# Attention and two MoE layers on one core: the first two batches' attention as single-engine parts in a planned order

## Chip, core and metric

One Trainium2 chip, one core. The time is the device time of one execution in microseconds; the metric is the median of the runs. The engines are PE (TensorE matmuls), ACT (ScalarE), DVE (VectorE), POOL (GpSimd) and SP (SyncE, which here issues the DMAs).

## What is computed

```python
def _attn_ref(q, k, v, M_prev, z_prev, beta):        # B, H, S, D = 4, 8, 576, 64
    scores = scale * np.matmul(q, k.transpose(0, 1, 3, 2))
    scores = np.where(causal, -1000000000.0, scores)
    scores = scores - scores.max(-1, keepdims=True)
    a = np.exp(scores)
    a /= a.sum(-1, keepdims=True) + 1e-09
    local = np.matmul(a, v)
    def phi(x):
        return np.where(x > 0, x, np.exp(x) - 1.0) + 1.0
    q_p = phi(q)
    mem_ret = np.einsum('bhsd,bhde->bhse', q_p, M_prev)
    mem_norm = np.einsum('bhsd,bhd->bhs', q_p, z_prev)[..., None] + 1e-06
    mem_out = mem_ret / mem_norm
    g = 1.0 / (1.0 + np.exp(-beta))[None, :, None, None]
    return (g * mem_out + (1 - g) * local).astype(np.float32)

def _moe_ref(x, w_gate, w_val, w_out):               # 2304 tokens, 512 -> 1536 -> 512
    g = x @ w_gate
    return (g * (1.0 / (1.0 + np.exp(-g))) * (x @ w_val) @ w_out).astype(np.float32)

def _moe2_ref(x, w_in, w_out):                       # 512 -> 2048 -> 512
    h = x @ w_in
    return (h * (1.0 / (1.0 + np.exp(-1.702 * h))) @ w_out).astype(np.float32)
```

The attention's output, with its heads side by side, is the first layer's x, and that layer's output the second's.

## The kernel before

A *pair* is two heads of one batch; there are 16, four to a batch. For a pair, the queries are cut into four tasks k: k 0 is the first two blocks of 128 queries, k 1 and 2 one block each, k 3 the last 64 queries of both heads. Each task passes all engines: PE multiplies scores into a PSUM tile `s`; DVE masks them and takes the maxima (`nm`); ACT takes the Exp with its sums (`sm`) into `p`; DVE inverts the sums; POOL scales `p` (the norm); PE transposes it into a PSUM tile `tp`; ACT copies that to `pt`. When all four are there, PE multiplies `pt` with v, and phi with the memory M, into `o` (`av`), ACT copies `o` to `xh`, DVE subtracts for `xl` (a value in two parts). Beside this runs phi of the pair's queries `nq`: Exp on ACT, a maximum with zero on POOL (L246), a sum on DVE (L247), the product with z on POOL (L249), a row sum and reciprocal on DVE, a division on POOL (L262), transposes on PE and a copy on ACT. `prep_q` scales qk on POOL (L234) and lays the last 64 queries into `qt`.

The program has three stages. First, the attention of batches 0 and 1 (`attn` with `alone`, 8 pairs) with PSUM tiles from both pools by turns. Second, `moe` over batches 0 and 1, both layers, with the attention of batches 2 and 3 (8 pairs) woven in at a rate worked out from costs; its result goes to DRAM. Third, `second`, both layers over batches 2 and 3.

A weight chunk of 128x512 goes through four steps, on ACT, DVE and POOL and back: load, `dec_one` (a 64-bit number's bits made into fp32), `split_one` (the same value in two parts, `wp`), and a copy to DRAM for the third stage, for most chunks with four sums of quarters. Chunk 0 is asked for by `ahead(0)` in the first stage, after its 60th step, which pulls six loads, four decodes and three splits; `moe` takes one chunk after the other with `next_w`.

The order of the program's text is not the order on the engines: the scheduler places each instruction on its engine by its own simulated timeline, and each engine then works in that order, waiting where an input is missing. `alone` steps are appended by the rule

```python
for x in "osten" if alone else "etnso":
    acts[x]()
```

where o is `av`, s scores, t the transposes, e the Exp and n the norm of neighbouring tasks.

## Time and profile before

| | us |
|---|---|
| median of 3 runs | 1113.54 |
| lowest and highest run | 1113.03, 1114.75 |
| profiled execution | 1110.42 |
| its span | 1108.6 |

The profiled execution is a single one; its span runs from the first to the last instruction. PE is busy 1053.2 us of it, POOL 637.8, DVE 694.0 and ACT 528.4. An engine's busy time leaves out its waits; a wait is shown with what ended it. A row of the timeline merges neighbouring instructions of one kind.

### The profile page before, as it was taken

How to read it: one execution, taken by the hardware profiler on the slowest of the kernel's cores; microseconds unless marked ns; L12 is line 12 of the kernel's file. 1: busy time of each engine (PE TensorE's matmuls, PEld its weight loads, DVE VectorE, ACT ScalarE, POOL GpSimd, SP SyncE). 2: the span in 40 equal slices, each digit the busy share in tenths (PEclk: the TensorE clock that was granted, in tenths of full speed). 3: DMA queues.
4: the chain of work that ended last, by engine and by line, in shares of the span. 5: the costliest groups of instructions: out<-in, count | busy, mean ns of one | idle time of the engine just before them, and what ended most of it. 6: DMA issues, size and time to landing. Idle time of an engine off the chain costs nothing.

```text
span 1108.6 us, 19842 instructions
## 1 busy us (share of the span) xinstructions
PE 1053.2 (95%) x7664; PEld 972.6 (88%) x7664; DVE 694.0 (63%) x1077; ACT 528.4 (48%) x1075; POOL 637.8 (58%) x650
## 2 busy tenths in 40 slices
PE   4768889999999999999999999999999999999998
PEld 3445459999989998899999999999999999999998
DVE  6777646844765857674846644880754869175563
ACT  4666645544544554666636444442432436343230
POOL 8899755666767657575654633481753818152421
PEclk8888989999999999999999999999999999999999
DMA  5355322454354353343453417422122222222102
GB/s 204 95 185 158 103 60 74 165 173 157 121 182 156 114 186 134 119 171 122 151 162 105 170 57 257 167 100 77 67 90 88 75 86 84 78 87 89 53 24 86
DMA packets 46719, 133.94 MB, mean 121 GB/s; under 512 B 7584, under 2 KB 10400, under 8 KB 46624
## 3 DMA queue, kind: packets, MB, share of 16 engines
q1 hardware_dynamic: 46480, 132.67, 35.7%
q8 instruction: 60, 0.98, 0.4%
q14 instruction: 35, 0.29, 0.1%
q10 hardware_dynamic: 144, 0.00, 0.0%
HBM read 92.54 MB, written 40.11 MB: 120 GB/s over the span
## 4 chain that ended last, share of the span: by engine, by line
PE 55%; DVE 2%; POOL 1%; issue 1%; DMA 0%; SPq 0%; ACT 0%; POOLq 0%; ACTq 0%
PE m L86 51%; PE o L86 2%; PE s L86 1%; POOL wb L598 1%; PE tp L350 1%; DMA out<-ot 0%; SPq L813 0%; POOL wp L153 0%; DVE hl L468 0%; DVE phi L247 0%; DVE wa L142 0%; PE tp L362 0%; DVE xl L621 0%; POOL nq L246 0%; PE tphi L269 0%
## 5 line engine op out<-in xcount | busy, mean ns | idle before, releaser
L86 PE MATMUL m<-hh,wp 128*128 128x288 f32 x1792 | 313.0, 297 | 2.8 <-DVE acc L520 2.4
L86 PEld LDWEIGHTS m<-hh,wp 128*128 128x128 f32 x1792 | 262.3, 189 | 12.9 <-issue 5.9
L86 PE MATMUL m<-xh,wp 128*128 128x288 f32 x1280 | 237.3, 300 | 2.1 <-DVE acc L520 1.3
L598 POOL TENSOR_TENSOR wb<-raw,wb 128x256 fp32r<-128x256 f32 x140 | 126.5, 920 | 191.0 <-ACT wb L597 185.9
L86 PEld LDWEIGHTS m<-xh,wp 128*128 128x128 f32 x1280 | 191.1, 189 | 12.7 <-issue 4.8
L86 PE MATMUL m<-hl,wp 128*128 128x288 f32 x896 | 191.1, 296 | 0.0
L145 POOL TENSOR_TENSOR wa<-wa,wr 128x512 uint32<-128x512 uint32 x68 | 90.0, 1324 | 117.1 <-issue 65.2
L86 PEld LDWEIGHTS m<-hl,wp 128*128 128x128 f32 x896 | 143.7, 188 | 1.3 <-issue 1.3
L86 PE MATMUL m<-xl,wp 128*128 128x288 f32 x640 | 137.0, 296 | 0.0
L153 POOL TENSOR_TENSOR wp<-wa,wp 128x512 fp32r<-128x512 f32 x68 | 93.0, 1368 | 55.6 <-ACT wp L152 54.9
L86 PE MATMUL m<-xh,wb 128*128 128x288 f32 x640 | 119.0, 296 | 0.0
L86 PEld LDWEIGHTS m<-xl,wp 128*128 128x128 f32 x640 | 103.1, 189 | 0.0
L86 PEld LDWEIGHTS m<-xh,wb 128*128 128x128 f32 x640 | 96.9, 189 | 0.0
L597 ACT CAST wb<-raw 128x256 fp32r<-128x256 f32 x140 | 55.6, 404 | 78.8 <-PE m L86 77.2
L306 ACT ACTIVATE p<-s,nm 128x128 f32<-128x128 f32 (+3 forms) x128 | 66.0, 525 | 52.0 <-DVE nm L289 40.5
L86 PE MATMUL m<-th,wb 128*128 128x288 f32 x480 | 90.3, 296 | 0.0
L326 POOL TENSOR_SCALAR p<-p,sm 128x128 f32<-128x128 f32 (+3 forms) x128 | 76.0, 610 | 20.1 <-DVE sm L322 6.9
L139 DVE TENSOR_SCALAR wa<-wa 128x512 f32<-128x512 f32 x68 | 36.9, 544 | 74.8 <-ACT wa L138 73.7
L144 ACT ACTIVATE wr<-w 128x512 uint32<-128x512 uint16 x68 | 45.9, 675 | 71.9 <-POOL wa L145 71.5
L468 DVE TENSOR_TENSOR hl<-u,hh 128x576 fp32r<-128x576 f32 x56 | 59.2, 1056 | 28.2 <-ACT hh L467 27.7
L86 PEld LDWEIGHTS m<-th,wb 128*128 128x128 f32 x480 | 73.1, 189 | 0.0
L86 PE MATMUL m<-xl,wb 128*128 128x288 f32 x320 | 68.6, 296 | 0.0
(143 smaller groups left out, 1833.9 us busy)
## 6 DMA issues: line engine op xcount, KB each, us to landing
w<-w SPq DMA_DIRECT2D x40, 512.0 KB, 3.6
raw<-w SPq DMA_DIRECT2D x20, 896.0 KB, 4.6
w<-wo SPq DMA_DIRECT2D x28, 512.0 KB, 3.6
w<-wp SPq DMA_DIRECT2D x28, 512.0 KB, 2.7
wp<-w SPq DMA_DIRECT2D x28, 512.0 KB, 3.5
w<-sums SPq DMA_DIRECT2D x20, 512.0 KB, 2.9
qk<-qk SPq DMA_DIRECT2D x32, 288.0 KB, 3.7
nq<-nat SPq DMA_DIRECT2D x16, 320.0 KB, 3.5
```

The source lines that it names most:

```text
L86: nc.tensor.matmul(o, w, x, start=start, stop=stop)
L139: nc.vector.tensor_scalar(a, a, HIGH, LOW, op0=ALU.min, op1=ALU.max)
L144: nc.scalar.activation(r, rest, AF.Copy, scale=2.0 ** -13)
L145: nc.gpsimd.tensor_tensor(au, au, r, op=ALU.add)
L153: nc.gpsimd.tensor_sub(wp[:, 1], t, f(wp[:, 0]))
L306: mark[0] = nc.scalar.activation(p[:, j, c:c + n], s[:, j, c:c + n], AF.Exp, bias=nm[:, x, j:j + 1], accum_out=sm[:, x, j:j + 1])
L326: nc.gpsimd.tensor_scalar(p[:, j, c:c + n], p[:, j, c:c + n], sm[:, x, j:j + 1], 1.0, op0=ALU.mult, op1=ALU.mult)
L350: nc.tensor.transpose(t[:, j, c:c + 128], p[:, j, c:c + 128], ident)
L468: nc.vector.tensor_sub(hl, t, f(hh))
L597: nc.scalar.copy(wb[:, 0], src)
L598: nc.gpsimd.tensor_sub(wb[:, 1], src, f(wb[:, 0]))
```

## The change

The attention's functions are cut into parts that each run on one engine (`scores`, `top`, `expo`, `recip`, `norm`, `turn`, `turned`, and so on). For batches 2 and 3 (`beside`) the parts are called in the old sequence. For batches 0 and 1 (`alone`) each part becomes an entry with an engine, a duration, a priority, the parts it follows and the buffers that it takes and gives; `ordered` makes one order of them, starting on each free engine the ready part of lowest priority number; `pinned` then ties each instruction to the one before it on its engine, so that the scheduler can't move it. The first five weight loads and decodes and three splits are entries too, of the last priorities, and the loads wait for pair 7's first scores.

Some work differs as well, in all 16 pairs. phi's negative part is made by two ACT passes, exp(-relu(-q)), and its sum with max(q, 0) by one DVE pass; POOL's pass over nq is gone. The copy of `pz` moves from DVE to ACT. The reciprocals use a table `il2` without a broadcast. In the first stage `s` tiles have one PSUM pool and all others the second; qk has three buffers instead of two, p six instead of three, pt two of its own. The memory is laid out in stages: the first stage's tiles are freed before `up`, `hpool` and the second stage's are laid in their place; the decoding's tiles lie at the other end.

```diff
-            nc.scalar.activation(e, q, AF.Exp)
-            nc.gpsimd.tensor_scalar(q, q, 0.0, None, op0=ALU.max)
-            nc.vector.scalar_tensor_tensor(e, e, 1.0, q, op0=ALU.min, op1=ALU.add)
+            nc.scalar.activation(e, q, AF.Relu, scale=-1.0)
+            nc.scalar.activation(e, e, AF.Exp, scale=-1.0)
...
+            nc.vector.scalar_tensor_tensor(e, q, 0.0, e, op0=ALU.max, op1=ALU.add)
...
-                nc.vector.tensor_copy(pzs[i % 2][64:128], t[64:128, 1, 0:128].rearrange("p (j q) -> p j q", j=2))
+                nc.scalar.copy(pzs[i % 2][64:128], t[64:128, 1, 0:128].rearrange("p (j q) -> p j q", j=2))
...
+        def psum(name, score=False):
+            if alone and not score:
+                return ps_m.tile([128, 2, 512], F32, tag="m", name=name)
+            return ps_s.tile([128, 2, 512], F32, tag="s", name=name)
...
+    def ordered(ops, stock):
...
+            ready = sorted(
+                (key, n) for n, (e, us, key, after, takes, gives, do) in left.items()
+                if all(x in end and end[x] + (LAG.get(ops[x][0], 0.2) if ops[x][0] != e else 0.0) <= now for x in after))
+            for key, n in ready:
+                e, us, _, _, takes, _, _ = ops[n]
+                if e in used or any(stock[x] < 1 for x in takes):
+                    continue
...
+    def pinned(ops, order):
+        last = {}
+        for n in order:
+            traced = nc.cur_bb.bb.instructions
+            n0 = len(traced)
+            ops[n][6]()
+            for ins in nc.cur_bb.bb.instructions[n0:]:
+                prev = last.get(ins.engine)
+                if prev is not None:
+                    tc.add_manual_dep(
+                        ins, prev, mybir.DependencyInfo(mybir.DependencyClass.NoSync, mybir.DependencyReason.DATA),
+                        reason="order")
+                last[ins.engine] = ins.name
...
+                op("scores", w, (i, k), "PE", (0.95, 0.9, 1.06, 1.1)[k], (("prep_q", i),), ("s",),
+                   ("qk", "qt") if k == 3 else ())
+                op("top", w, (i, k), "DVE", (1.8, 1.4, 1.65, 1.0)[k], (("scores", i, k),))
...
+        wait = ("scores", NP - 1, 0)
...
+        for i in range(5):
+            key = 4 * NP + i
+            op("w", key, (i,), "SP", 0.4, (wait,), ("big",), do=load)
...
-    for n, (_, fn, args) in enumerate(attn(pairs[:2 * HP], True, direct)):
-        fn(*args)
-        if n == 60:
-            with tc.issue_after(mark[0].ins):
-                ahead(0)
-    steps = attn(pairs[2 * HP:], False, stage)
+    with tc.tile_pool(name="atta", bufs=1) as atta:
+        alone(atta, pairs[:2 * HP], direct)
+    up = ctx.enter_context(tc.tile_pool(name="up", bufs=3))
+    hpool = ctx.enter_context(tc.tile_pool(name="hpool", bufs=8))
...
+    steps = beside(attb, pairs[2 * HP:], stage)
```

How the order moves, at three places. PE before, around the output of pair 5 in the first stage (`s` scores, `tp` transposes of `p`, `o` output; 64x288 and the like are the parts of `o` from `pt`):

```order
L350 MATMUL tp<-ident,p 128x128 x8
L86 MATMUL s<-qk 128x384 x2
L86 MATMUL o<-ph,mz_97 128x288 x2
L362 MATMUL tp<-ident,p 128x128 x4
L363 MATMUL tp<-ident,p 128x128
L86 MATMUL s<-qk 128x512 x2
L350 MATMUL tp<-ident,p 128x128 x6
L86 MATMUL o<-pz_99,v 64x64 x2
L86 MATMUL o<-ptx,v 64x192 x2
L86 MATMUL o<-ptx,v 64x288 x6
```

PE now, around the outputs of pairs 3 and 4:

```order
L84 MATMUL s<-qk 128x384 x2
L380 MATMUL tp<-ident,p 128x128 x6
L84 MATMUL s<-qk 128x512 x2
L380 MATMUL tp<-ident,p 128x128 x8
L384 MATMUL tp<-ident,p 128x128 x4
L385 MATMUL tp<-ident,p 128x128
L84 MATMUL s<-qk,qt_87 128x288 x2
L380 MATMUL tp<-ident,p 128x128 x6
L84 MATMUL o<-ph,mz_88 128x288 x2
L84 MATMUL o<-pz_90,v 64x64 x2
L84 MATMUL o<-pt,v 64x192 x2
```

Before, the first two matmuls of `o` (with `ph` and mz) came ahead of the last transposes and of scores, and the rest of `o` after them; now `o` comes in one piece, and scores of the next pair and transposes stand between one `o` and the next.

ACT before, in the first stage at the weights' first decoding (L138, L144 decode, L152 splits, L306 is the Exp):

```order
L306 ACTIVATE p,sm<-s,nm 128x128 x2
L306 ACTIVATE p,sm<-s,nm 128x256 x2
L306 ACTIVATE p,sm<-s,nm 128x384 x2
L138 ACTIVATE wa<-w_565 128x512
L144 ACTIVATE wr<-w_565 128x512
L138 ACTIVATE wa<-w_567 128x512
L144 ACTIVATE wr<-w_567 128x512
L138 ACTIVATE wa<-w_569 128x512
L364 COPY ptx<-tp 128x2x4x64
L144 ACTIVATE wr<-w_569 128x512
L152 CAST wp<-wa 128x512
```

ACT now, at the end of the first stage (L343 and L347 are the Exp of pair 7, L142 and L143 decode, L425 makes `xh`, the others copy `tp`):

```order
L343 ACTIVATE p,sm<-s,nm 128x512 x2
L347 ACTIVATE p,sm<-s,nm 128x576
L142 ACTIVATE wa<-w_1202 128x512
L143 ACTIVATE wr<-w_1202 128x512
L142 ACTIVATE wa<-w_1204 128x512
L143 ACTIVATE wr<-w_1204 128x512
L425 CAST xh<-o 128x576
L398 COPY pt<-tp 128x2x3x128
L142 ACTIVATE wa<-w_1212 128x512
L143 ACTIVATE wr<-w_1212 128x512
L400 COPY pt<-tp 128x2x4x128
L402 COPY pt<-tp 128x2x4x64
```

The first decoding moved from among the third pair's Exps to behind the last pair's.

SP before, early in the first stage (w loads a weight, mz loads M into a tile that the pair two before it reads):

```order
L218 DMA nq<-nat 128x640
L226 DMA v<-nat 128x640
L229 DMA mz_97<-mem 64x64 x2
L119 DMA w_565<-w 128x1024
L119 DMA w_567<-w 128x1024
L119 DMA w_569<-w 128x1024
L218 DMA nq<-nat 128x640
```

SP now, at the end of the first stage (`w_92` is a weight's copy to DRAM; the last mz, qk, zb and nq are pair 8's):

```order
L117 DMA w_1202<-w 128x1024
L117 DMA w_1204<-w 128x1024
L117 DMA w_1212<-w 128x1024
L251 DMA mz_88<-mem 64x64 x2
L117 DMA w_1363<-w 128x1024
L176 DMA w_92<-wa 128x512
L117 DMA w_1395<-w 128x1024
L117 DMA w_1441<-w 128x1024
L251 DMA mz_89<-mem 64x64 x2
L229 DMA qk<-qk 128x576 x2
L238 DMA zb<-z 128x512
L240 DMA nq<-nat 128x640
```

The first weights' loads moved behind all eight pairs' loads, and those of pair 8 behind them.

POOL before, where the first stage ends (L333 and L326 norms, L234 and L237 prepare a pair's qk, L249 multiplies phi by z, L145 decodes, L153 splits):

```order
L234 TENSOR_SCALAR qk<-qk 128x576
L249 TENSOR_TENSOR nq<-phi,zb 128x640
L333 TENSOR_SCALAR p<-p,sm 128x576
L237 COPY qt_95<-qk 64x64 x2
L262 TENSOR_TENSOR phi<-phi,nrm 128x640
L326 TENSOR_SCALAR p<-p,sm 128x128 x2
L326 TENSOR_SCALAR p<-p,sm 128x256 x2
L153 TENSOR_TENSOR wp<-wa,wp 128x512
L145 TENSOR_TENSOR wa<-wa,wr 128x512
L153 TENSOR_TENSOR wp<-wa,wp 128x512
```

POOL now, in the same place, after the last norms (L258 and L261 prepare a pair's qk, L279 multiplies phi by z, L152 decodes, L171 splits, L180 to L183 sums):

```order
L152 TENSOR_TENSOR wa<-wa,wr 128x512 x2
L171 TENSOR_TENSOR wp<-wa,wp 128x512 x2
L180 TENSOR_TENSOR sums<-wa 128x256
L181 TENSOR_TENSOR sums<-sums,wa 128x256
L182 TENSOR_TENSOR sums<-wa 128x256
L183 TENSOR_TENSOR sums<-wa,sums 128x256
L152 TENSOR_TENSOR wa<-wa,wr 128x512
L258 TENSOR_SCALAR qk<-qk 128x576 x2
L261 COPY qt_86<-qk 64x64 x2
L279 TENSOR_TENSOR nq<-phi,zb 128x640
L261 COPY qt_87<-qk 64x64 x2
L171 TENSOR_TENSOR wp<-wa,wp 128x512
```

Before, the preparation of pairs 8 and 9 stood among the last norms of the stage, and four weights had been split ahead of them; now two weights are split after all norms, and the third weight's split stands behind that preparation.

## Rows read from the trace of the kernel before

**Rows 1.** The page's first part (busy us, share of the span, instructions) for PE, and its chain that ended last, by engine.

```profile
PE 1053.2 (95%) x7664; PEld 972.6 (88%) x7664; DVE 694.0 (63%) x1077; ACT 528.4 (48%) x1075; POOL 637.8 (58%) x650
...
PE 55%; DVE 2%; POOL 1%; issue 1%; DMA 0%; SPq 0%; ACT 0%; POOLq 0%; ACTq 0%
```

**Rows 2.** The table by stretches. Columns: the stretch and its length in us; busy us and instruction count of PE, PEld, DVE, ACT and POOL; granted TensorE clock; DMA share; GB/s.

```profile
20.00:158.00 138.00, 103.74 (x639) 64.45 (x638) 99.55 (x197) 87.45 (x218) 118.50 (x140) 0.87 0.41 125
158.00:200.00 42.00, 42.00 (x310) 38.88 (x310) 24.55 (x38) 18.88 (x37) 23.45 (x22) 0.97 0.23 71
200.00:665.00 465.00, 460.50 (x3402) 425.67 (x3401) 293.96 (x482) 246.97 (x475) 286.69 (x278) 1.00 0.43 144
101.95:149.21 47.26, 38.48 (x259) 24.43 (x259) 31.27 (x69) 29.99 (x80) 34.94 (x47) 0.93 0.32 98
116.91:131.66 14.75, 11.95 (x89) 7.51 (x88) 9.83 (x23) 10.35 (x28) 11.15 (x15) 1.00 0.34 105
```

**Rows 3.** PE's waits from 20 to 158 us: who waited for whom, us in total, times, longest.

```profile
PE o L86 <- ACT p L306: 14.6, 6, 4.5
PE tp L362 <- POOL p L333: 8.8, 5, 3.8
```

**Rows 4.** PE's timeline: start us, us, instructions merged by kind and count, and in brackets the idle time before them and what ended it. An `x8` of 64-row tiles is four matmuls of the program.

```profile
116.91 0.82 PE L350 MATMUL tp<-ident,p 128*128 128x128 f32 x6
...
124.23 1.24 PE L86 MATMUL o<-ph,mz 128*128 128x288 f32 x4 [2.46 <-ACT p L306]
...
131.66 1.14 PE L86 MATMUL s<-qk,qt 128*128 128x288 f32 x4
...
153.59 0.93 PE L86 MATMUL s<-qk 64*128 64x128 f32 x8
...
158.49 0.83 PE L86 MATMUL m<-xh,wp 128*128 128x288 f32 x2
...
162.85 2.83 PE L86 MATMUL o<-ptx,v 128*64 128x192 f32 x28
```

**Rows 5.** Groups of instructions from 101.95 to 149.21 us (three pairs), shapes kept apart: line, engine, operation, output<-inputs, shapes, count | busy us, mean ns of one | idle time before them and what ended it.

```profile
L246 POOL TENSOR_SCALAR nq<-nq 128x640 f32<-128x640 f32 x3 | 5.4, 1812 | 0.9 <-ACT phi L245 0.7
...
L295 DVE TENSOR_REDUCE nm<-s 128x1 f32<-128x576 f32 x3 | 2.3, 757 | 0.1
...
L245 ACT ACTIVATE phi<-nq 128x640 f32<-128x640 f32 x3 | 2.3, 756 | 0.0
...
L320 DVE SCALAR_TENSOR_TENSOR sm<-sm,il 128x4 f32<-128x4 f32 x3 | 2.1, 684 | 0.5 <-ACT p L306 0.5
...
L358 ACT COPY pt<-tp 128x1024 f32<-128x1024 f32 x2 | 2.0, 1012 | 0.0
...
L385 ACT CAST xh<-o 128x576 fp32r<-128x576 f32 x3 | 1.9, 641 | 0.4 <-PE o L86 0.3
...
L356 ACT COPY pt<-tp 128x768 f32<-128x768 f32 x2 | 1.6, 824 | 0.3 <-PE tp L350 0.3
...
L364 ACT COPY pt<-tp 128x512 f32<-128x512 f32 x2 | 1.2, 586 | 0.6 <-PE tp L363 0.5
...
L365 DVE COPY pz<-tp 64x128 f32<-64x128 f32 x3 | 0.9, 295 | 0.1
```

**Rows 6.** The first 20 us: the table by stretches for 14 to 20 (columns as above), then one row each of the timelines of SP's queue, ACT, POOL and PE.

```profile
14.00:20.00 6.00, 2.98 (x9) 2.30 (x10) 4.40 (x13) 3.23 (x12) 5.84 (x9) 0.50 0.42 144
6.14 0.58 SPq L218 DMA_DIRECT2D nq<-nat  x1
11.25 0.74 ACT L245 ACTIVATE phi<-nq 128x640 f32<-128x640 f32 x1 [2.61 <-DMA nq<-nat]
10.57 1.65 POOL L234 TENSOR_SCALAR qk<-qk 128x576 f32<-128x576 f32 x1
17.02 0.47 PE L350 MATMUL tp<-ident,p 128*128 128x128 f32 x1 [6.38 <-POOL p L326]
```

**Rows 7.** Groups of instructions from 160 to 665 us, the weights' decoding and splitting among them (columns as in rows 5).

```profile
L153 POOL TENSOR_TENSOR wp<-wa,wp 128x512 fp32r<-128x512 f32 x62 | 85.2, 1374 | 47.3 <-ACT wp L152 46.7
...
L145 POOL TENSOR_TENSOR wa<-wa,wr 128x512 uint32<-128x512 uint32 x61 | 80.7, 1323 | 115.2 <-issue 65.2 <-DVE sm L320 22.6 <-DVE wa L142 19.3
...
L142 DVE SCALAR_TENSOR_TENSOR wa<-w,wa 128x512 uint32<-128x512 uint32 x61 | 47.5, 779 | 1.1
...
L138 ACT ACTIVATE wa<-w 128x512 f32<-128x512 f32 x61 | 41.2, 675 | 45.0 <-POOL wp L153 44.8
...
L152 ACT CAST wp<-wa 128x512 fp32r<-128x512 f32 x62 | 38.2, 616 | 18.6 <-PE m L86 18.6
...
L139 DVE TENSOR_SCALAR wa<-wa 128x512 f32<-128x512 f32 x61 | 32.5, 533 | 73.7 <-ACT wa L138 72.6 <-DMA v<-nat 0.6
...
L164 POOL TENSOR_TENSOR sums<-wa 128x256 f32<-128x256 f32 x17 | 13.9, 821 | 0.0
```

**Rows 8.** From the page: the norm's passes on POOL in all 16 pairs (columns as in rows 5), and the loads of qk (line, engine, operation, count, KB each, median us from issue to landing); then POOL's timeline after the boundary.

```profile
L326 POOL TENSOR_SCALAR p<-p,sm 128x128 f32<-128x128 f32 (+3 forms) x128 | 76.0, 610 | 20.1 <-DVE sm L322 6.9
...
qk<-qk SPq DMA_DIRECT2D x32, 288.0 KB, 3.7
...
171.91 1.27 POOL L153 TENSOR_TENSOR wp<-wa,wp 128x512 fp32r<-128x512 f32 x1 [10.81 <-ACT wp L152]
```

**Rows 9.** DVE's timeline: a product on sm while the norms have not begun.

```profile
14.81 0.15 DVE L320 SCALAR_TENSOR_TENSOR sm<-sm,il 128x4 f32<-128x4 f32 x1
```

More of the change, by code (lines that the diff above doesn't have):

```diff
@@ L146, in dec_one, with two, three @@
+        def two():
+            nc.vector.tensor_scalar(a, a, HIGH, LOW, op0=ALU.min, op1=ALU.max)
+            nc.vector.tensor_scalar(au, au, 3, 0x3FFFFFFF, op0=ALU.logical_shift_left, op1=ALU.bitwise_and)
+            nc.vector.scalar_tensor_tensor(au, top, 0xC0000000, au, op0=ALU.bitwise_and, op1=ALU.bitwise_or)
+        def three():
+            nc.gpsimd.tensor_tensor(au, au, r, op=ALU.add)
         raws[i] = a
+        return one, two, three
     def split_one(i):
         upto("dec", i + 1, dec_one)
+        for stage in split_stages(i):
+            stage()
@@ L170, in ahead @@
+        return one, two
     def ahead(i):
@@ L388, in av, with beside @@
             done()
+        names = locals()
+        return {n: names[n] for n in (
+            "load_qk load_nq load_v prep_q phi_exp phi_sum phi_z phi_norm phi_div phi_turn phi_out scores top "
+            "expo recip norm turn turned av x_hi x_lo").split()}
+    def beside(pool, pairs, dest):
+        a = attention(pool, pairs, False, dest)
+        NP = len(pairs)
         tasks = [(i, k) for i in range(NP) for k in range(4)]
         NTK = len(tasks)
-        st, ptk = {}, {}
         steps = []
-        def add(cost, fn, *args):
-            steps.append((cost, fn, args))
@@ L398, in do_scores, with add @@
[L398 to L420 removed]
+        def add(cost, *what):
+            steps.append((cost, [(a[n], args) for n, *args in what]))
@@ L430, in attn @@
-            for x in "osten" if alone else "etnso":
-                acts[x]()
+            if 0 < t <= NTK:
+                add(0.0, ("expo", *tasks[t - 1]))
+            if 2 <= t < NTK + 2:
+                add(T_COST[tasks[t - 2][1]], ("turn", *tasks[t - 2]), ("turned", *tasks[t - 2]))
+            if 0 < t <= NTK:
+                add(0.0, ("recip", *tasks[t - 1]), ("norm", *tasks[t - 1]))
+            if t < NTK:
+                add(S_COST[k], ("scores", i, k), ("top", i, k))
+            if t >= 3 and tasks[t - 3][1] == 3:
+                x = tasks[t - 3][0]
+                add(3.9, ("av", x), ("x_hi", x), ("x_lo", x))
@@ L771, in tile_attention_moe_moe @@
     nc.vector.tensor_scalar(ig, ig, 1.0, None, op0=ALU.add)
+    for x in range(2):
+        nc.vector.tensor_copy(il2[:, :, x], il)
     for j in range(2):
```

355 lines of the change are left out of this document (211 added, 144 removed).

## The prediction

> **What bounds the kernel now.** I began with the page's busy shares and its chain of waits: PE is busy 95% of the span and carries 55% of the chain, nearly all of it the MoE matmuls [rows 1]. So work saved on another engine is worth something only where PE waits. The table by stretches says where that is [rows 2]. From 158 to 200 us PE is busy 42.00 of 42 us, from 200 to 665 us 460.50 of 465. From 20 to 158 us, in the first two batches' attention, it is busy 103.74 of 138 at a mean granted clock of 0.87: 34.3 us of idle PE, and PE work done in part at the lower of two clock levels. The change can win only there, and not more than some 45 us.
>
> Why PE waits there is in its waits [rows 3]: 14.6 us before the output matmul `o` on ACT, 8.8 us before the transposes of the last block on POOL. No engine is full: over three whole pairs without any weight decoding (101.95 to 149.21, 15.75 us each) PE is busy 38.48 of 47.26 us, POOL 34.94, DVE 31.27, ACT 29.99 [rows 2]. It is the order that makes 15.75 us of a pair. The row at 124.23 shows how: PE stands 2.46 us in front of `o` with transposes queued behind it [rows 4].
>
> **The floor after the change.** From 116.91 to 131.66 exactly one pair's PE instructions start, and PE is busy 11.95 us there at clock 1.00 [rows 2, 4]. POOL has 34.94 / 3 = 11.65 per pair and loses the pass over nq, 1.81 [rows 5]: 9.84. DVE has 10.42 and loses the copy of pz, 0.30: 10.1. ACT has 10.0 and gains the Relu pass and that copy. The trace has no Relu; bounds are 0.64 and 0.82, ACT passes over 576 and 768 elements, and I take the 0.76 of the Exp on the same tile. For the copy I take DVE's 0.30; ACT's 0.59 for 128x512 is the upper bound [rows 5]. ACT: 11.1. So PE leads with 11.95 and ACT follows at 93% of that. The other edits (il2 filled at the start by two tiny copies on an idle DVE; deeper rings for qk, p and pt) add nothing to a busy engine.
>
> **The ramp.** PE starts with the first pair's scores and then idles 6.38 us; from 14 to 20 us its clock is 0.50; the first transpose starts at 17.02 [rows 6]. The new order keeps that chain. The second nq load, issued at 6.14, is used at 11.25, and ACT needs it for two passes before the first Exp of scores; pair 1's qk is scaled from 10.57 [rows 6]; then POOL does the phi products, a division and the first norm in a row, with the nq passes gone. I take 17.5 us for the first transposes, 0.5 later than now for the second ACT pass.
>
> **The stretch.** 8 x 11.95 = 95.6, less 3.9 for the scores done in the ramp (a third of a pair), plus 2.0 for a restart at half clock (14 to 20 holds 2.98 us of PE [rows 6], the new order puts more there): 93.7 us of PE work. PE will not be full. The nearest rows are 81%, the three pairs in the old order, and 100%, 158 to 200 us, where all inputs lie ready [rows 2]. I choose 93%, nearer to the upper: the two waits that made most of the gaps are in-order waits, and PE's new order runs up to three score tiles ahead and no longer splits `o` around other work; but ACT at 93% of PE's load can't serve every slot. 93.7 / 0.93 = 100.8; the ends are 93.7 and 115.7.
>
> **The tail.** After the last scores of pair 7 PE still has one `o` (1.24 + 2.83 [rows 4]) and 19 transposes (0.82 for six): 6.7 us. Beside it go DVE's maximum, 0.76, an Exp like that of phi, 0.76, and then on ACT, by the new order, three weight decodes of two passes (6 x 0.675), x_hi (0.64) and four PSUM copies (0.82, 1.01, 0.59, 0.30) before the last `o` can start [rows 5, 7]: 8.9. So 2.2 us idle. The stage ends at 17.5 + 100.8 + 2.2 = 120.5 us (113.4 to 135.4).
>
> **What it is compared with.** Now the first MoE matmul starts at 158.49, with the last `o` (2.83 from 162.85) still to come and 0.9 us of pair 8's scores (153.59) already done [rows 4]. For the same PE work the old boundary is 158.49 + 2.83 - 0.93 = 160.4. Gain 39.9 us.
>
> **What comes back.** The five weight decodes that lay in the middle of this stage come at its end, and pair 8's loads queue among theirs on SP. Let E be the stage's end. Weights 0 and 1 are loaded well ahead; each then takes ACT 1.35, DVE about 1.8 (0.53, a like pass, 0.78), POOL 1.32, ACT 0.62, POOL 1.37 [rows 7], and they are ready about 1 us before and 1 us after E, where PE needs the second at E + 5.9. Weight 2's last pass stands on POOL behind four sums (0.82 each) and behind the scaling of pairs 8 and 9. Their loads follow on SP a mem load into a tile that pair 7's `o` still reads: they leave from E + 2 on and land, 3.7 us each [rows 8], near E + 6 and E + 8. Then come the second scaling, qt, a phi product, qt and the pass, some 5.6 us of POOL: weight 2 is whole near E + 14, and PE wants it after two weights and pair 8's first score tiles, also near E + 14. Weight 3 (E + 21) is level with its use as well. POOL has 10.81 us of idle there now [rows 8]; it will have none. I take 2 us of new stall, between 0 and 8 (two loads later by as much as one takes). After that PE is full as before [rows 2], and ACT's added 1.1 us per pair lie beside it, where ACT is busy 246.97 of 465 us; uncovered they would cost 9 us.
>
> Gain 39.9 - 2 = 37.9. The profiled execution took 1110.42 us, so 1072.5 after. The runs' median, 1113.54, lies 3.1 above it: I predict **1076 us**.
>
> **Where the Trainium skill speaks.** PE's pause before 17.02 is followed by 0.50 of clock from 14 to 20 us [rows 6]. The Trainium skill's page "TensorE: Matmul & The Clock Gate" (Part 1: The HAM clock gate) says that the array is throttled by default and that activity releases it. By that rule each gap left in the new order costs twice, which is the mechanism of the first rival.
> DVE's product on sm takes 0.15 us at 14.81 [rows 9] and 0.68 on average in the three pairs [rows 5]. The Trainium skill's page "GPSIMD Engine Reference" (1. Specifications) says that POOL shares its SBUF interface with VectorE and contends with instructions of two SBUF inputs. The slow rows agree; by that rule a denser order makes DVE's work longer, the second rival.
>
> **Rivals.**
> 1. *The gaps stay, and the low clock with them.* In-order waits on the two `m` buffers, with six users per pair, leave a pair at the 15.75 us of the three pairs, whose clock is 0.93 [rows 2]. 93.7 us are 7.84 pairs: 123.5, end 143.2, gain 160.4 - 143.2 - 2 = 15: 1098. For it: ACT is nearly as loaded as PE. Against: the old gaps stand before two named waits.
> 2. *DVE becomes the bound.* If each of the four sm products and their reciprocals takes 0.5 us more: 10.1 + 2 = 12.1 per pair, level with PE. Two full engines instead of one at a share of 88%: 106.5, 5.7 later than forecast: 1082.
> 3. *The weights come too late.* The whole 8 us of stall: 1082, and 1085 with a spell of half clock after it.
> 4. *Slower than now.* One pinned order makes one late load stop all that is behind it. On SP the z row of batch 1 is issued ahead of pair 4's qk and must wait until POOL has multiplied pair 3's phi by z; in POOL's order pair 4's scaling then follows after eight norm passes (8 x 0.61 = 4.9 us [rows 8]) and a division, while the load needs its issue and 3.7. If such a ring formed in every pair, the gain is nothing at (158.4 - 19.7) / 7.84 = 17.7 us a pair, and at 19 us the time is 1124. Against it: that wait is met once, and the work before the scaling about covers it.
>
> **How the numbers follow.** Forecast (PE bound, share 88 to 100%, stall 0 to 4): 0.70, with a range of its own from 1063 to 1083. Rival 1, and what lies between it and 1083: 0.15. Rivals 2 and 3: 0.07. Rival 4: 0.06, of which 0.05 is slower. Better than 1063: 0.02. The range 1063 to 1096 reaches to rival 1's near half and so holds some 0.84. A difference of 0.2% (2.2 us) is what a measurement can tell from none: faster 0.93, same 0.02, slower 0.05.
>
> **What would show it.** Right: the first MoE matmul near 121 us; PE's share from 20 to 115 us above 88% at a clock of 0.97 or more; `o` no longer waiting for an Exp; at most 2 us of idle PE in the 40 us after the boundary. Wrong: a clock under 0.95 in that stretch (rival 1), DVE busier than PE (rival 2), PE waiting before the first weights' matmuls on POOL's wp (rival 3), PE waiting on pair 4's scaling (rival 4), or a MoE part, from its first matmul to the end, that is not within 3 us of the 948 us that 1108.6 - 160.4 makes it now.

## The result and the profile after

| | before | after |
|---|---|---|
| median, us | 1113.28 (1112.48 to 1114.75) | 1087.49 (1085.24 to 1088.78) |
| profiled execution, its span | 1110.42, 1108.6 | 1085.24, 1083.4 |
| after / before | | 0.9765 (0.9743 to 0.9786) |

The change is faster by 2.35%, within the forecast range of 1063 to 1096 and 11.5 us above the point 1076. The page's first part and its chain, as in [rows 1] (busy us, share, instructions):

```profile
PE 1039.8 (96%) x7664; PEld 967.1 (89%) x7664; DVE 690.2 (64%) x1063; ACT 542.1 (50%) x1107; POOL 612.6 (57%) x634
...
PE 54%; DVE 3%; DMA 1%; ACT 1%; POOL 1%; issue 1%; SPq 0%; DVEq 0%; POOLq 0%
```

PE's busy time fell by 13.4 us (the same 7664 matmuls, at a mean granted clock of 0.998 instead of 0.980), the span by 25.2; the rest is idle time of PE. The table by stretches says where, with the columns of [rows 2]: the stage from its first transposes to the first MoE matmul, its middle, the 72.5 us behind it, and the long part:

```profile
22.52:127.48 104.96, 90.70 (x669) 59.22 (x668) 77.62 (x166) 84.59 (x215) 74.48 (x103) 1.00 0.31 96
34.60:113.40 78.80, 71.39 (x522) 46.48 (x522) 58.47 (x130) 62.16 (x165) 57.56 (x84) 1.00 0.31 97
127.48:200.00 72.52, 64.44 (x444) 58.99 (x442) 58.60 (x84) 40.43 (x83) 64.05 (x60) 0.98 0.59 195
200.00:640.00 440.00, 437.90 (x3236) 406.13 (x3237) 274.79 (x448) 241.45 (x465) 267.69 (x263) 1.00 0.43 145
```

Three readings. In the middle of the stage PE is busy 71.39 of 78.80 us (91%) at clock 1.00, against 81% at 0.93 in the old order's three pairs [rows 2]. From 200 us on it is full, as before. Between, 8.1 of 72.5 us are idle; in the 72.5 us behind the first MoE matmul of the kernel before it was 0.7.

PE's waits from 22 to 128 us, beside [rows 3] (who waited for whom, us in total, times, longest):

```profile
PE s L84 <- ACT p L343: 6.4, 9, 1.6
PE tp L380 <- issue: 1.9, 2, 1.6
PE tp L380 <- DVE xl L430: 1.7, 1, 1.7
PE tp L380 <- ACT ph L303: 1.1, 1, 1.1
PE tp L380 <- POOL qk L258: 1.0, 1, 1.0
PE o L84 <- ACT pt L400: 0.7, 1, 0.7
```

The 14.6 us of `o` behind an Exp and the 8.8 us of the last transposes behind POOL are gone. What is left is one small wait met often: scores for a free `s` tile, which an Exp still reads. PE's timeline at the ends of the stage, beside [rows 4, 6]:

```profile
18.43 2.08 PE L84 MATMUL s<-qk 64*128 64x512 f32 x4 [9.18 <-ACT p L343]
...
22.52 0.79 PE L299 MATMUL tphi<-ident,phi 128*128 128x128 f32 x5
...
121.10 1.07 PE L380 MATMUL tp<-ident,p 128*128 128x128 f32 x8 [1.73 <-DVE xl L430]
...
123.39 1.24 PE L84 MATMUL o<-ph,mz 128*128 128x288 f32 x4 [0.68 <-ACT pt L400]
...
127.48 0.53 PE L84 MATMUL m<-xh,wp 128*128 128x288 f32 x2
```

The first transposes start at 22.52, where I had said 17.5, and the first MoE matmul at 127.48, where I had said 120.5; no `o` is left behind it. From there to the end are 1083.4 - 127.48 = 955.9 us, which I call the MoE part below; before it was 948.2 by the count of the prediction. So the profiled execution is 12.7 us above the forecast 1072.5: 5.0 in the ramp, 2.0 in stretch and tail, 5.7 in the MoE part.

**The ramp.** DVE's timeline from 9 to 18 us:

```profile
9.70 0.83 DVE L273 SCALAR_TENSOR_TENSOR phi<-nq,phi 128x640 f32<-128x640 f32 x1 [3.40 <-ACT phi L268]
13.06 1.84 DVE L273 SCALAR_TENSOR_TENSOR phi<-nq,phi 128x640 f32<-128x640 f32 x1 [2.54 <-ACT phi L268]
14.82 0.69 DVE L327 TENSOR_TENSOR s<-s,bound 128x512 f32<-128x512 f32 x1
15.54 1.02 DVE L329 TENSOR_REDUCE nm<-s 128x2 f32<-128x256 f32 x2
```

PE's first scores ended at 9.25, but DVE masks them only at 14.82: in its order phi's sum of pair 1 stands in front, and that waits for ACT, which waits for pair 1's nq. SP issued nq at 5.56, ACT took it at 11.52: 6.0 us, for which the plan's table has 2.0 (`LAG`). The PE row at 18.43 is the end of that: 9.18 us idle before the third task's scores.

**Behind the boundary.** DVE's and ACT's timelines, and PE's waits from 127 to 200 us:

```profile
131.50 0.79 DVE L146 TENSOR_SCALAR wa<-wa 128x512 f32<-128x512 f32 x1 [2.48 <-ACT wa L142]
...
138.56 0.83 DVE L273 SCALAR_TENSOR_TENSOR phi<-nq,phi 128x640 f32<-128x640 f32 x1 [4.00 <-ACT phi L268]
139.31 0.75 DVE L645 SCALAR_TENSOR_TENSOR u<-u,m 128x576 f32<-128x576 f32 x1
140.14 1.77 DVE L146 TENSOR_SCALAR wa<-wa 128x512 f32<-128x512 f32 x1
```
```profile
137.02 0.74 ACT L267 ACTIVATE phi<-nq 128x640 f32<-128x640 f32 x1 [4.44 <-DMA nq<-nat]
```
```profile
PE m L84 <- DVE u L654: 3.5, 3, 1.8
PE m L84 <- DVE u L645: 3.2, 5, 1.5
PE s L84 <- ACT p L347: 1.4, 1, 1.4
```

PE doesn't wait for a weight (`wp`), as the prediction had it, but for DVE's `u`, which has to empty the PSUM tile of the product before. And DVE is not free for it: it stands 4.0 us before pair 8's phi, whose nq landed late, and then works without a pause, with decoding passes between the `u`.

### The profile page after: what moved, and what is told of

It reads as the page before. It is cut to its first block, busy times and chain, and to the rows that moved or that the text cites. A ratio compares the mean times of both kernels' runs of the same rounds, so it can differ in the third digit from the quotient of the medians.

```text
span 1083.4 us, 19848 instructions
## 1 busy us (share of the span) xinstructions
PE 1039.8 (96%) x7664; PEld 967.1 (89%) x7664; DVE 690.2 (64%) x1063; ACT 542.1 (50%) x1107; POOL 612.6 (57%) x634
## 4 chain that ended last, share of the span: by engine, by line
PE 54%; DVE 3%; DMA 1%; ACT 1%; POOL 1%; issue 1%; SPq 0%; DVEq 0%; POOLq 0%
PE m L84 50%; PE o L84 1%; PE s L84 1%; DVE hl L615 1%; DMA raw<-w 1%; PE tp L380 1%; DMA xr<-x 0%; DVE u L685 0%; ACT hh L614 0%; POOL wa L152 0%; DVE xl L768 0%; DMA x<-st 0%; DVE wa L149 0%; POOL p L368 0%; POOL wp L171 0%
## 5 line engine op out<-in xcount | busy, mean ns | idle before, releaser
L84 PE MATMUL m<-xh,wp 128*128 128x288 f32 x1280 | 239.9, 302 | 6.7 <-DVE u L645 3.2
L152 POOL TENSOR_TENSOR wa<-wa,wr 128x512 uint32<-128x512 uint32 x68 | 92.7, 1364 | 105.3 <-issue 48.5
L171 POOL TENSOR_TENSOR wp<-wa,wp 128x512 fp32r<-128x512 f32 x68 | 93.5, 1375 | 40.6 <-ACT wp L168 40.2
L146 DVE TENSOR_SCALAR wa<-wa 128x512 f32<-128x512 f32 x68 | 42.2, 620 | 77.3 <-ACT wa L142 76.8
L343 ACT ACTIVATE p<-s,nm 128x128 f32<-128x128 f32 (+3 forms) x128 | 66.1, 530 | 32.6 <-DVE nm L329 30.5
L84 PE MATMUL s<-qk 64*128 64x128 f32 (+3 forms) x256 | 54.2, 487 | 23.3 <-ACT p L343 15.0
L142 ACT ACTIVATE wa<-w 128x512 f32<-128x512 f32 x68 | 46.1, 677 | 58.2 <-POOL wp L171 52.9
L143 ACT ACTIVATE wr<-w 128x512 uint32<-128x512 uint16 x68 | 46.1, 677 | 53.6 <-POOL wa L152 53.2
```

The lines of the kernel that those rows point to most:

```text
L84: nc.tensor.matmul(o, w, x, start=start, stop=stop)
L142: nc.scalar.activation(a, top.bitcast(F32), AF.Abs)
L143: nc.scalar.activation(r, rest, AF.Copy, scale=2.0 ** -13)
L146: nc.vector.tensor_scalar(a, a, HIGH, LOW, op0=ALU.min, op1=ALU.max)
L152: nc.gpsimd.tensor_tensor(au, au, r, op=ALU.add)
L171: nc.gpsimd.tensor_sub(wp[:, 1], t, f(wp[:, 0]))
```

## The experiments

All times are medians in us, the ratio is to the kernel before, timed on the same chip beside it, with its 95% interval; the chips differ between rows, so the ratios compare better than the medians. "First" is the first MoE matmul of the profiled execution, "MoE part" its span less that, "u" PE's waits for DVE's `u` in the 72.5 us behind it, "decoded" the chunks whose decoding was complete before it (POOL's last pass, L152).

| kernel | median | ratio | first | MoE part | u | decoded |
|---|---|---|---|---|---|---|
| before | 1113.28 | | 158.49 | 950.1 | 0.7 | 7 |
| after | 1087.49 | 0.9765 (0.9743 to 0.9786) | 127.48 | 955.9 | 6.7 | 2 |
| phi alone | 1106.58 | 0.9946 (0.9926 to 0.9966) | 159.91 | | 0.5 | 7 |
| no ties | 1092.76 | 0.9826 (0.9788 to 0.9863) | 141.35 | 948.7 | 4.6 | 7 |
| weights early | 1092.19 | 0.9818 (0.9786 to 0.9851) | 141.82 | 950.0 | 3.2 | 7 |
| shallow buffers | 1101.25 | 0.9894 (0.9877 to 0.9912) | 151.16 | 946.8 | 1.5 | 5 |
| minimum on DVE | 1085.98 | 0.9756 (0.9738 to 0.9775) | 132.14 | 952.8 | 8.5 | 3 |
| DVE's order | 1082.47 | 0.9734 (0.9705 to 0.9763) | 131.90 | 948.6 | 3.1 | 4 |
| less DVE decoding | 1080.69 | 0.9708 (0.9694 to 0.9722) | 127.38 | 951.4 | 4.6 | 2 |
| less POOL | 1086.59 | 0.9759 (0.9742 to 0.9777) | 127.66 | 957.2 | 9.5 | 2 |
| nq first | 1084.96 | 0.9750 (0.9724 to 0.9776) | 126.56 | 956.4 | 8.5 | 2 |
| nq first, less DVE | 1083.94 | 0.9721 (0.9687 to 0.9755) | 127.52 | 954.7 | 6.4 | 2 |
| less DVE and POOL | 1082.87 | 0.9722 (0.9688 to 0.9756) | 127.59 | 953.3 | 6.6 | 2 |
| three edits | 1081.16 | 0.9720 (0.9697 to 0.9743) | 122.06 | 956.0 | 7.0 | 2 |

(Before, 1.9 us of attention matmuls stood behind the first MoE matmul, hence 950.1 here and 948.2 in the prediction; with phi alone `o` stands behind it too, and the MoE part can't be compared.)

**phi alone.** The kernel before, with the new phi in all 16 pairs and nothing else:

```diff
-            nc.scalar.activation(e, q, AF.Exp)
-            nc.gpsimd.tensor_scalar(q, q, 0.0, None, op0=ALU.max)
-            nc.vector.scalar_tensor_tensor(e, e, 1.0, q, op0=ALU.min, op1=ALU.add)
+            nc.scalar.activation(e, q, AF.Relu, scale=-1.0)
+            nc.scalar.activation(e, e, AF.Exp, scale=-1.0)
+            nc.vector.scalar_tensor_tensor(e, q, 0.0, e, op0=ALU.max, op1=ALU.add)
```

> The kernel before, with phi alone changed, in all 16 pairs: two ACT passes in place of one on ACT and one on POOL. Theory (order, not POOL's load, made a pair 15.75 us): gain of 0 to 6 us, 1107 to 1113. Rival (POOL's pass over nq held the first stage): gain of 12 us or more, 1101 or less.

0.54% (0.34 to 0.74), some 6 us of the change's 26, come from the cheaper phi, the upper end of the theory's 0 to 6. The rest lies in the other edits together: the order, the buffers, the two PSUM pools, the copy of pz and `il2`.

**No ties.** The plan and the buffers of the change, but the scheduler may move instructions:

```diff
-                if prev is not None:
+                if False:
```

> The changed kernel, with the parts written in the planned order but the instructions not tied to their predecessors, so that the scheduler places them. Theory (the order on the engines is what gained): much of it is lost, first MoE matmul at 140 to 155, time 1098 to 1112. Rival (the cut into parts, the buffers and the order of writing are enough): within 3 us of 1087.

Neither: 1092.8, some 5 us lost of 26. The first transposes come at 20.83, but the first MoE matmul 14 us later. From 34.60 to 113.40 us, against the row above:

```profile
34.60:113.40 78.80, 64.65 (x434) 41.32 (x434) 64.85 (x131) 60.86 (x156) 74.87 (x97) 0.96 0.41 131
```

POOL is busy 74.87 of 78.80 us instead of 57.56: without ties the scheduler put seven weights' decoding into the stage, four of them into this stretch. So what the ties keep seems to be mostly one thing: they hold the decoding at the stage's end. The next run, which keeps the ties and moves the decoding alone, ends in the same place.

**Weights early.** The same by the plan itself, with ties: the loads wait for pair 3's scores, with priorities among the pairs':

```diff
-        wait = ("scores", NP - 1, 0)
+        wait = ("scores", 3, 0)
...
-            key = 4 * NP + i
+            key = 16 + 3 * i
             op("w", key, (i,), "SP", 0.4, (wait,), ("big",), do=load)
```

> The changed kernel, with the five weights' loads waiting for pair 3's first scores instead of pair 7's, and their priorities spread over pairs 4 to 7. Theory (the 8.1 us that PE idles in the 72.5 us after the boundary come from decoding that is caught up there on a full POOL and DVE): that idle falls to 2 or less, the first MoE matmul comes 5 to 8 us later, time 1085 to 1090. Rival (the idle comes from pairs 8 and 9, whose preparation starts in the same place, or from the memory's reuse): idle stays at 6 or more and the time rises by the 5 to 8 us, to 1092 to 1096.

It ends as the run without ties did: stage 14.3 us longer, twice what I expected, MoE part 5.9 us shorter. The idle behind the boundary falls from 8.1 to 3.6 us, between the two expectations, and the time is the rival's. The two runs give the exchange rate: decoding inside the stage, where POOL then fills (71.29 of 78.80 us here), costs about twice what it saves behind it.

**Shallow buffers.**

```diff
-            t = new("qk", [128, 2, S], 3 if deep else 2)
+            t = new("qk", [128, 2, S], 2)
...
-            p = ps[i, k] = new("p", [128, 2, 512], 6 if deep else 3)
+            p = ps[i, k] = new("p", [128, 2, 512], 3)
...
-        order, us = ordered(ops, {"qk": 3, ..., "p": 6, ...
+        order, us = ordered(ops, {"qk": 2, ..., "p": 3, ...
```

> The change with the old depth of buffers in the first stage: qk two instead of three, p three instead of six (pt stays). Theory (PE's share of 91% in 34 to 113 us rests on scores and Exps running ahead of the transposes, for which p and qk have room): with three p each Exp waits for an older transpose, s tiles are freed later, PE's waits for s grow from 6.4 us; first MoE matmul 5 to 12 us later than 127.5, time 1091 to 1098. Rival (the order alone does it; the two s tiles bind and not p): first MoE matmul within 2 us of 127.5, time 1085 to 1090.

More than expected: 13.8 us, with the first MoE matmul 23.7 us later and the MoE part 9.1 us shorter. PE's waits for `s` grow from 6.9 to 12.8 us (the Exps of all tasks). In the middle of the stage PE's share falls from 91% to 83%, and the plan, with fewer free buffers, now sets two splits and four sums on POOL ahead of the last norms, before which PE stands 6.96 us:

```profile
34.60:113.40 78.80, 65.21 (x457) 42.55 (x459) 52.83 (x118) 55.58 (x145) 55.06 (x78) 0.96 0.27 81
```
```profile
139.69 1.97 PE L380 MATMUL tp<-ident,p 128*128 128x128 f32 x8 [6.96 <-POOL p L368]
```

So the gain of the order stands on room to run ahead. Without it an order from the same planner is worth half, though a part of what is lost is the decoding that it moved ahead of the norms. The old order with the new buffers and PSUM pools was not run: what the room alone is worth isn't shown.

**Minimum on DVE.** ACT relieved of one phi pass per pair (in the plan it is a part of its own, on DVE):

```diff
-            nc.scalar.activation(e, q, AF.Relu, scale=-1.0)
-            nc.scalar.activation(e, e, AF.Exp, scale=-1.0)
+            nc.vector.tensor_scalar(e, q, 0.0, None, op0=ALU.min)
+            nc.scalar.activation(e, e, AF.Exp)
```

> In all 16 pairs phi's first pass, the Relu on ACT, becomes a minimum with zero on DVE (0.7 us); the Exp and the sum stay as they are in the change. ACT's load in the stage goes from 84.6 to about 78, DVE's from 77.6 to about 83. Theory (PE's idle 14% of the stage is waiting for ACT's Exp, 'PE s from ACT p', because ACT is nearly as full as PE): those waits fall from 6.4 us to 3 or less, first MoE matmul 3 to 6 us earlier, and the first pair's phi ends 0.8 us sooner; time 1081 to 1085. Rival (the load of ACT does not matter, the waits are those of a round trip through DVE, ACT and two score tiles): nothing in the stage, and DVE's added 0.7 us per pair makes the first chunks after the boundary later; time 1087 to 1091.

The waits for `s` behind that Exp do fall, from 6.4 to 2.4 us. But the first MoE matmul comes 4.7 us later and the time is that of the change within its error: the plan came out with decoding ahead of pair 7's last norms, and PE stood 6.03 us before them. The middle of the stage:

```profile
34.60:113.40 78.80, 72.67 (x512) 46.84 (x512) 56.35 (x130) 58.40 (x157) 55.48 (x78) 0.96 0.32 99
```

Its 72.67 us are not more work than the 71.39 of the change: they hold 512 matmuls instead of 522, at a mean granted clock of 0.96 instead of 1.00. So what ACT's load costs in the stage isn't shown by this run. The next one speaks against a large part, for there the same waits fall to 3.3 us with ACT's work as it was.

**DVE's order.** One more dependency in the plan, pair 1's phi sum behind pair 0's second maximum:

```diff
-            op("phi_sum", t - 0.5, (i,), "DVE", 0.85, (("phi_exp", i),))
+            op("phi_sum", t - 0.5, (i,), "DVE", 0.85,
+               (("phi_exp", i),) + ((("top", 0, 1),) if i == 1 else ()))
```

> The changed kernel, with one dependency more in its plan: DVE's phi sum of pair 1 comes after the maxima of pair 0's first two tasks instead of ahead of them. Theory (the plan counts 2.0 us from a load's issue to its use, the trace shows 6.0 for pair 1's nq, so DVE stands 2.5 us before that sum with pair 0's scores ready): the first Exp of scores starts near 13.1 us instead of 16.66, PE's first transposes near 18.5 instead of 22.52, the first MoE matmul near 124 instead of 127.5, time 1083 to 1085. Rival (the loads and POOL's preparation bound the start whatever DVE does): first transposes stay within 1 us of 22.5, time 1086 to 1089.

The ramp is settled: transposes 4.1 us earlier, by one instruction's place.

```profile
18.40 0.71 PE L299 MATMUL tphi<-ident,phi 128*128 128x128 f32 x5
```

The time fell by 5.0 us, a little more than expected, but not by the way expected: the first MoE matmul came 4.4 us later and the MoE part was 7.3 us shorter, since the plan, with other times at its start, set two chunks ahead of the last norms. POOL and PE there:

```profile
115.60 2.69 POOL L171 TENSOR_TENSOR wp<-wa,wp 128x512 fp32r<-128x512 f32 x2
...
121.63 0.74 POOL L372 TENSOR_SCALAR p<-p,sm 128x576 f32<-128x576 f32 x1
```
```profile
122.42 1.12 PE L384 MATMUL tp<-ident,p 128*128 128x128 f32 x4 [5.17 <-POOL p L372]
```

Two splits and four sums stand before the last norm, and PE waits 5.17 us for it. Behind that wait the granted clock is 0.54 (123.55 to 131.50), and the 28 matmuls of the last `o` with `pt` take 4.47 us instead of 2.83.

**Less DVE decoding.** For chunks 3 to 15 two of DVE's three decoding passes are left out:

```diff
-            nc.vector.tensor_scalar(a, a, HIGH, LOW, op0=ALU.min, op1=ALU.max)
-            nc.vector.tensor_scalar(au, au, 3, 0x3FFFFFFF, op0=ALU.logical_shift_left, op1=ALU.bitwise_and)
+            if not 3 <= i < 16:
+                ...
```

> For weight chunks 3 to 15 two of DVE's three decoding passes are left out (the limits and the shift; their values are then wrong), 1.0 us of undisturbed DVE time per chunk; nothing else is changed. Theory (what the MoE's start loses, 8.1 us of idle PE in the 72 us after the first MoE matmul, is DVE, which decodes the late weights beside a busy POOL, so that u comes late): that idle falls to 3 us or less, PE's waits for DVE's u from 6.7 us to 2 or less, DVE's busy time in those 72 us from 58.6 to about 46; time 1081 to 1084, the first MoE matmul unmoved within 1 us. Rival (POOL, or pair 8's late preparation, holds it): PE's idle stays within 1.5 us of 8.1, time 1086 to 1089.

The time falls by 6.8 us (the span of the profiled execution by 4.6), PE's idle from 8.1 to 4.8, the waits for `u` from 6.7 to 4.6: in the theory's direction, but over half of the waits stay, although DVE is busy 48.39 instead of 58.60 us. DVE's amount of work is a part of the cause and not the whole.

```profile
127.38:199.90 72.52, 67.73 (x470) 63.19 (x469) 48.39 (x66) 42.47 (x81) 68.17 (x64) 0.98 0.65 222
```

**Less POOL.** Its four sums for every second chunk from 4 to 15 left out:

```diff
-                nc.gpsimd.tensor_add(m[:, 2], a2[:, 0], a2[:, 1])
-                ...
+                if 3 <= i < 16:
+                    nc.sync.dma_start(out=kept[i - 1][:, 2:4], in_=a1)
+                    nc.sync.dma_start(out=kept[i - 1][:, 4:6], in_=a2)
+                    ...
```

> For weight chunks 4 to 15 the four sums of quarters of every second chunk on POOL (3.3 us per two chunks) are left out, and the quarters themselves are copied to DRAM in their place (the third stage's inputs are then wrong); nothing else is changed. Theory (POOL's only part is that DVE's passes take longer while POOL is busy; DVE is what PE waits for): POOL's busy time in the 72 us after the first MoE matmul falls by about 13 us to 51; DVE's passes come nearer to their undisturbed times, PE's idle falls from 8.1 to 4 to 6 us; time 1083 to 1086. Rival (POOL itself is the bound after the boundary, through wp and the norms of pairs 8 and 9, as the prediction had it): idle falls to 2 us or less, time 1080 to 1082. A third: neither, idle within 1 us of 8.1.

None of the three, and nearest the last: POOL's busy time falls from 64.05 to 52.66 us and nothing is gained; the waits for `u` even rise, to 9.5, and PE's idle to 12.3. The edit also adds copies to DRAM and moves the scheduler's order, so it doesn't show that POOL's work is free. But relieving POOL did not help, and in the change PE waited for no `wp` at all: this step of my prediction is refuted.

```profile
127.66:200.18 72.52, 60.20 (x426) 55.40 (x425) 56.12 (x81) 39.18 (x75) 52.66 (x49) 1.00 0.63 207
```

**nq first.** Pair 8's first step is called ahead of the MoE, nq its first load, and the first stage has its own mz tiles:

```diff
-        add(0.0, ("load_qk", 0), ("load_nq", 0), ("prep_q", 0), ...
+        add(0.0, ("load_nq", 0), ("load_qk", 0), ("prep_q", 0), ...
...
+        own = [new(f"mz{x}", [128, 128], 1) for x in range(2)] if alone else mzs
...
+    for fn, args in steps.pop(0)[1]:
+        fn(*args)
     for c in moe(xh, xl):
```

> Pair 8's loads are brought forward: its first step stands ahead of the MoE's first weights in the program, nq is its first load, and the eight pairs of the first stage have mz tiles of their own, so that pair 9's mem load waits for no output matmul in SP's queue. Nothing is left out. In the change nq of pair 8 is issued at 130.83 and ACT takes it at 137.02; DVE, in order, stands 4.0 us in front of pair 8's phi sum (138.56), and decoding passes and u queue behind it. Theory (this late load, not the amount of POOL or DVE work alone, sets off the late u): nq leaves near 127, is used near 133, DVE's 4 us wait falls to 1 or less, PE's idle in the 72 us after its first MoE matmul falls from 8.1 to 4 to 5.5; first MoE matmul unmoved within 1 us; time 1083 to 1085. Rival (DVE is simply full with late decoding, so its 4 us of wait are taken up elsewhere): idle 7 to 9 us, time 1086 to 1089.

The median is the theory's, but by its interval it can't be told from the change, and the spans of the profiled executions differ by 0.4 us; the idle, 8.6 us, is the rival's. ACT's and PE's timelines show why:

```profile
134.77 0.74 ACT L272 ACTIVATE phi<-nq 128x640 f32<-128x640 f32 x1 [3.68 <-DMA nq<-nat]
135.41 0.63 ACT L649 ACTIVATE u<-m 128x576 f32<-128x576 f32 x1
```
```profile
136.89 0.54 PE L84 MATMUL m<-xh,wp 128*128 128x288 f32 x2 [3.68 <-DVE u L650]
```

nq, issued at 127.73, still took 7.0 us, and the scheduler now had pair 8's phi in front of the Tanh of `u` on ACT. The wait was not taken away, it moved to where it holds `u` directly.

**nq first with less DVE decoding, and less of both.** The edits above, two by two.

> The run with pair 8's loads brought forward and the run without two of DVE's decoding passes for chunks 3 to 15, in one kernel (so that those chunks' values are wrong here too). Alone the first left PE's idle at 8.6 us in the 72.5 us after the first MoE matmul and the second brought it to 4.8. Theory (DVE's work sets the idle and, once DVE has slack, the 4.9 us that it still stood in front of pair 8's phi sum is what is left): idle 1.5 to 3.5 us, MoE part 948 to 950, time 1077 to 1080. Rival (what is left has nothing to do with pair 8's loads): idle 4.3 to 6, MoE part 951 to 953, time 1080 to 1082.

> For chunks 3 to 15 both the two DVE decoding passes and the four POOL sums of every second chunk are left out (values wrong, quarters copied in place of sums). Theory (two engines share the blame: with DVE relieved, POOL's work is what is left of the idle): idle 1 to 3 us in the 72.5 us after the first MoE matmul, MoE part 947 to 949.5, time 1076 to 1079. Rival (POOL matters neither alone nor with DVE relieved): idle 4 to 6 us as without the DVE passes alone, MoE part 951 to 953, time 1080 to 1082.

Both miss their theories: waits for `u` of 6.4 and 6.6 us, MoE parts of 954.7 and 953.3, the second just above its rival's. Each is compared with the kernel that differs by one edit. Leaving out the DVE passes shortens the MoE part by 4.5 us alone (955.9 to 951.4), by 1.7 with nq first (956.4 to 954.7) and by 3.9 without POOL's sums (957.2 to 953.3). The other two edits shorten it in no pair: nq first adds 0.5 and 3.3 us, leaving out the sums 1.3 and 1.9. Each edit moves the scheduler's order behind the boundary, and some wait for `u` of 1 to 4 us appears at another place. A part is clock: with nq first and less DVE work, PE's waits of 3.31 and 3.11 us for `u` (ended at 137.48 and 156.96) were followed by granted clocks of 0.60 from 138 to 141 and 0.72 from 156 to 162 us, and the 72.5 us have a mean of 0.95 instead of 0.98.

**Three edits.** DVE's order, nq first, and the weights' loads behind pair 7's second scores, by which POOL's order has all decoding behind the last norms again:

```diff
-        wait = ("scores", NP - 1, 0)
+        wait = ("scores", NP - 1, 1)
```

> Three edits together, nothing left out: pair 1's phi sum behind pair 0's second maximum, pair 8's loads brought forward as in the run beside this one, and the weights' loads waiting for pair 7's second scores instead of its first, so that on POOL no decoding pass stands ahead of the stage's last norms (with the first edit alone two did, and PE stood 5.2 us before the last transposes). Theory: first transposes near 18.4, first MoE matmul at 122 to 124.5 (the ramp's 4 us carry through), MoE part from there 951 to 955; span 1074 to 1079, time 1076 to 1081, faster than both. Rival (the weights' first decoding has to be paid before or after that matmul, whatever the order): first MoE matmul at 122 to 125 but a MoE part of 957 to 961; time 1082 to 1087.

The stage came as the theory had it, first transposes at 18.50; the MoE part lay between the two, and so did the time. PE's timeline, and the 72.5 us behind the first matmul:

```profile
122.06 0.53 PE L84 MATMUL m<-xh,wp 128*128 128x288 f32 x2
```
```profile
122.06:194.58 72.52, 65.06 (x457) 60.82 (x455) 62.13 (x83) 40.48 (x77) 62.50 (x58) 0.98 0.61 204
```

At 1081.16 it has the lowest median of those that leave nothing out, ratio 0.9720 against 0.9765 for the change, their intervals just touching. From the run with DVE's order alone (0.9734) it can't be told. In its stage the waits for `s` behind the Exp of the first three tasks are 3.3 us, and the middle is busy 73.31 of 78.80 us, 93%, at clock 1.00.

## Why the prediction was right, and where it was not

The time lies in the range, but not in the forecast's own part of it, 1063 to 1083 for a share of 88 to 100% and a stall of 0 to 4 us. The share was 86% and the loss behind the boundary 7.7 us; the time fell where the prediction gave 0.15 to rival 1 and what lies short of it, and rival 1 did not occur. What held is the mechanism in the stage: the two in-order waits went, and PE ran at clock 1.00.

1. **The floor and the long part held.** PE is the busiest engine of the stage (90.70 busy us against 84.59 of ACT, which is 93% of it as forecast), the clock is 1.00, and from 200 us on PE is full although ACT's passes were added there.
2. **The ramp was mis-sized**: 17.5, measured 22.52. I said that the new order keeps the old chain, from nq and ACT to the first norm; I had not walked DVE's queue, where pair 1's phi stands before pair 0's maxima. Shown: moving that one sum gives 18.40.
3. **The share was mis-sized.** 93% in the stretch, with the tail's idle time 93.7 of 103.0 us or 91%; measured 90.70 of 104.96, 86%, and 91% in the middle. The two big waits went as argued. Left are short ones for `s` tiles, and the start and end of the stage. ACT's load was my reason against a full PE; how much of the rest it makes stays open, for with DVE's order, nq and the loads' start changed and ACT's work as it was, the middle reached 93%. That stretch and tail together were only 2.0 us over is luck in part: the PE work was 3.0 us less than the 93.7 of the prediction. 2.0 of these are its restart at the lower clock, which fell into the ramp: there two tasks' scores took 2.08 and 2.29 us, later 1.13 and 1.24. The buffers, which I priced at nothing, hold the order up: with the old depth the time is 13.8 us longer.
4. **What comes back was mis-sized, within its bounds**: 2 us taken, 0 to 8 given, 7.7 measured in the MoE part. The place was right, pair 8's late loads and the late weights; the engine was wrong. I named POOL's last pass of the weights, and PE waited for DVE's `u`. Weight 2's last pass even ended near 17 us behind the boundary (on POOL, 144.23) instead of 14, and PE did not wait for it. DVE's queue, where decoding and pair 8's phi stand in front of `u`, had no term in the sum, so that 7.7 lies within bounds set for another wait is luck. Nor did five weights' decoding lie in the old stage but seven (POOL's L145, 50.09 to 95.78 us); the change has two of them done at the boundary. Rival 3 had the price but the same wrong engine.
5. **The MoE part is longer where less was decoded ahead of it.** In the table, every kernel with four or more chunks decoded ahead of the first MoE matmul has a MoE part of 946.8 to 950.1 us; with two or three it is 951.4 to 957.2. In the 72.5 us behind the boundary DVE decodes ten chunks in the change and seven or eight before, and two of its three passes take longer there. By form, before and after, the first pass (L139, L146) and the third (L142, L149), which does not (busy us, mean ns); the second goes from 584 to 740 ns:

```profile
L142 DVE SCALAR_TENSOR_TENSOR wa<-w,wa 128x512 uint32<-128x512 uint32 x7 | 6.6, 947 | 0.1
...
L139 DVE TENSOR_SCALAR wa<-wa 128x512 f32<-128x512 f32 x8 | 5.0, 619 | 5.7 <-ACT wa L138 5.5
```
```profile
L146 DVE TENSOR_SCALAR wa<-wa 128x512 f32<-128x512 f32 x10 | 10.8, 1077 | 5.8 <-ACT wa L142 5.7
L149 DVE SCALAR_TENSOR_TENSOR wa<-w,wa 128x512 uint32<-128x512 uint32 x10 | 8.3, 834 | 0.1
```

   That the number of decoded chunks makes the difference is read across kernels that also differ otherwise, and not shown by an edit of it alone. Shown is that leaving out DVE's passes takes 1.7 to 4.5 us of it away, that leaving out POOL's sums takes none, and that an earlier issue of nq moves the wait without ending it. How the rest splits between late nq and decoding in front of `u` stays open.
6. The marks I had set: first MoE matmul near 121 us, measured 127.48 (wrong); `o` waits for no Exp (right); clock 1.00 (right); PE's share from 20 to 115 us 83.15 of 95.00, 87.5% where I wanted over 88 (just missed); idle PE in the 40 us behind the boundary 4.7, not 2 (wrong); MoE part 7.7 over, not within 3 (wrong).

Rival 4 did not form: SP waited 20.3 us before the z row, once, but PE waited only 1.0 us for a scaled qk. Rival 1 did not either (91% at 1.00 in the middle). Nor did each gap cost twice, as the prediction has it beside that rival: the gaps that PE met from 22.52 to 127.48 us, up to 1.73, were followed by no lower clock. Rival 2's engine was not the bound in the stage, but it was the one that PE waited for behind it. The row that the prediction sets against the slow products, 0.15 us at 14.81, is no row beside an idle POOL: POOL was in a pass over nq from 13.69 to 15.50. So the two rows do not show that POOL makes the difference.

## What to carry over

When a planned order replaces a scheduler's, walk each engine's queue from the first instruction with the loads' measured times: one instruction that waits in front of a ready one cost 4 us here, and a load time of 2 us in the plan's table was 6. Work that is pushed out of a stage to shorten it comes due at the next stage's start, so price that start by all engines that release PE, those that empty PSUM included. And a run-ahead order needs its buffers: count them as part of the change.
